# The minimum of the features on GpSimd, and the gate folded into the normaliser, in an attention-and-MoE kernel

## Chip, core and metric

The kernel runs on one core of a Trainium2 chip. The metric is the device time of one execution in microseconds (us); less is better. The engines are TensorE (PE; PEld is its weight load), VectorE (DVE), ScalarE (ACT), GpSimd (POOL) and SyncE (SP), whose queue issues the DMAs. Each engine runs its instructions in the order of its own queue, and waits on semaphores for the others.

## What is computed

Inputs: q, k, v of shape (4, 8, 576, 64), a memory matrix M_prev per batch and head (64 x 64), its normaliser z_prev, a gate beta per head, and four weight matrices. Cut to what matters:

```python
a = softmax(causal(q @ k.T / 8))
local = a @ v
q_p = np.where(q > 0, q, np.exp(q) - 1.0) + 1.0        # the features
mem_norm = (q_p * z_prev).sum(-1) + 1e-06
mem_out = (q_p @ M_prev) / mem_norm
g = 1.0 / (1.0 + np.exp(-beta))
x = g * mem_out + (1 - g) * local                       # (2304, 512)
out = ((x @ w1) * (x @ w2)) @ w3 @ w_out
```

The features are max(q, 0) + exp(min(q, 0)). The factor g / mem_norm is applied to the features of each token before they are multiplied with M_prev, and (1 - g) to the rows of the softmax.

## The kernel before

Two heads make a pair; the 4 batches have 16 pairs, and `pair_step(p)` handles one. The list ORDER gives the order in which a step is written down: transposes of the softmax rows of pair p (t1 to t4b, `t_mm`, L245 and L255 on PE, copied out of PSUM on ACT in L268), the product of rows and values (`pv_mm`, L277), `fin` (L288 on ACT and L289 on DVE, which split the result into a high and a low part), and then for the next pair the scores (`s_all`, L216 on PE; row minima with the mask on DVE, L193), the exponentials (L226, ACT) and the normalisation (L230, L231, L235 on DVE). At each F in ORDER, `Fill` writes down a share of other matmuls: in batch 0 the product of w3 and w_out (L423), in later batches the MoE of the batch before (`gemm1`, L473, and `gemm2`, L493). In `gemm1` ACT scales one product out of PSUM (L479), DVE multiplies the other to it (L482), ACT makes a rounded high part (L484) and POOL the low part (L485). The conversion of the weights from 64 bits (`conv_stages`: L310 on ACT, L314 and L315 on DVE, L322 on ACT, L323 on DVE) runs during batch 0 and the start of batch 1. After the last pair the MoE of the last batch runs alone.

The written order is not the order on the engines. A planner takes the instructions as written, gives each a place on its engine by priority and by the moment at which it reckons it ready, and adds the semaphores; instructions under `high_priority` come earlier. So the memory steps of a pair run well ahead of the place where they are written.

The memory steps of a pair, which the change touches:

- `load_qn` fetches q in token layout into the tile qn (L141 to L143; two buffers) and z (L146; two buffers) through SP's queue. A buffer of qn is free when the last features of its pair have been written (L178); one of z, when L160 has read it.
- `mem_a`: ACT makes e = relu(-q) (L152) and then e = exp(-e) (L153). The tile e is 128 x 640 and has one buffer.
- `mem_b`: DVE makes the features qn = max(q, 0) + e (L158), POOL makes e = qn * z (L160).
- `mem_c`: DVE sums e per token and head (L166, 128 x 10), adds 1e-6 (L167), takes the reciprocal (L168) and multiplies by the gate g_sb (L172); POOL multiplies the features with this, into the columns behind the softmax rows (L175 into sm0, L178 into smx), where the transposes of the next step take them. Both wait until the transposes of the pair before have read these columns.
- `copy_qd` (L120, POOL) copies q and k of the first rows when their DMA has landed.

Before the first pair, ACT and DVE make g_sb = 1 / (1 + exp(-beta)) (L604, L606, L607) and gi = 1 + exp(beta), which goes into the softmax sums.

Of the kernel before, what the change touches and what calls it, by code (L numbers as in the profile page):

```python
# [12 lines left out]
ACTF = mybir.ActivationFunctionType  # L13
ALU = mybir.AluOpType
# [28 lines left out]
def attention_moe_kernel(  # L43
# [13 lines left out]
    nc = tc.nc  # L57
# [35 lines left out]
    g_sb = const.tile([128, H], F32, name="g_sb")  # L93
# [55 lines left out]
    def mem_a(p):  # L149
        t = qn_t[p]  # L150
        e = mem_p.tile([128, 5, 2, D], F32, tag="e", name="e")
        nc.scalar.activation(out=e, in_=t, func=ACTF.Relu, scale=-1.0)  # L152
        nc.scalar.activation(out=e, in_=e, func=ACTF.Exp, scale=-1.0)  # L153
        stat["e", p] = e

    def mem_b(p):
# [5 lines left out]
    def mem_c(p):  # L162
        t, e = qn_t.pop(p), stat.pop(("e", p))
        n = st_p.tile([128, 5, 2, 1], F32, tag="n", name="n")
        nf = n.rearrange("p t h o -> p (t h) o")
        nc.vector.tensor_reduce(out=nf, in_=e.rearrange("p t h d -> p (t h) d"), axis=AX.X, op=ALU.add)  # L166
        nc.vector.tensor_scalar(out=n, in0=n, scalar1=1e-6, scalar2=None, op0=ALU.add)  # L167
        nc.vector.reciprocal(out=n, in_=n)  # L168
        h0 = 2 * p % H
        n3 = n.rearrange("p t h o -> p t (h o)")  # L170
        gb = g_sb[:, h0:h0 + 2].rearrange("p (o h) -> p o h", o=1).to_broadcast([128, 5, 2])
        nc.vector.tensor_tensor(out=n3, in0=n3, in1=gb, op=ALU.mult)  # L172
        for a in range(2):
            r = slice(64 * a, 64 * a + 64)
            nc.gpsimd.tensor_tensor(out=sm0[r, 64:128], in0=t[r, 0, a], in1=n[r, 0, a].to_broadcast([64, D]), op=ALU.mult)  # L175
        for k, lo, q, o in ((1, 0, 384, 192), (3, 512, 640, 576)):
            d = smx[:, :, lo:lo + 2 * q].rearrange("p a (k q) -> p k a q", q=q)[:, :, :, o:o + D]
            nc.gpsimd.tensor_tensor(out=d, in0=t[:, k:k + 2], in1=n[:, k:k + 2].to_broadcast([128, 2, 2, D]), op=ALU.mult)  # L178
# [364 lines left out]
    def pair_step(p, F):  # L543
# [23 lines left out]
            pv=(1, lambda: pv_mm(p)),  # L567
            fin=(1, lambda: fin(p)),
            ma=(nx, lambda: mem_a(p + 1)),
            mb=(nx, lambda: mem_b(p + 1)),  # L570
            qd=(nx, lambda: copy_qd(p + 1)),
            mc=(nx, lambda: mem_c(p + 1)),
        )
        for t in ORDER:
# [15 lines left out]
        out=mask[:, 448:576], in_=mask[:, 448:576], pattern=[[-1, 128]], compare_op=ALU.is_ge,  # L590
# [13 lines left out]
    nc.scalar.activation(out=g_sb, in_=beta_sb, func=ACTF.Exp, scale=-1.0)  # L604
    nc.scalar.activation(out=gi, in_=beta_sb, func=ACTF.Exp)
    nc.vector.tensor_scalar(out=g_sb, in0=g_sb, scalar1=1.0, scalar2=None, op0=ALU.add)  # L606
    nc.vector.reciprocal(out=g_sb, in_=g_sb)  # L607
    nc.vector.tensor_scalar(out=gi, in0=gi, scalar1=1.0, scalar2=None, op0=ALU.add)
    gp = gi.rearrange("p (j a) -> p j a", a=2)
    for k in range(4):  # L610
# [26 lines left out]
    load_v(0)  # L637
    load_qn(1)
    mem_a(0)
    mem_b(0)  # L640
    mem_c(0)
    F.slot()
    for b in range(B):
# [41 lines left out]
```

## Time and profile before

| | |
|---|---|
| median of 3 runs | 559.87 us (559.64 to 559.92) |
| the profiled execution | 558.28 us, its span 556.5 us |
| PE busy | 530.4 us, 95% of the span |
| DVE busy | 277.6 us, 50% |
| ACT busy | 269.0 us, 48% |
| POOL busy | 128.6 us, 23% |
| mean granted PE clock | 0.987 |

The span runs from the first to the last instruction of one profiled execution. A share of the span is an average over stages that have different limits. In rows of a timeline, "[x <-Y]" says that the engine stood idle for x us before the instruction and that Y ended the wait; a wait for several semaphores is put down to the one that came last. In rows by line, the two numbers behind the bar are the busy time in us and the mean of one instruction in ns. An instruction that the engine starts while the one before is still draining overlaps with it in these rows. Spans on POOL are rough.

### The profile page before, as it was taken

What the parts mean: (1) busy time and instruction counts of PE and PEld (TensorE: products, weight loads), DVE (VectorE), ACT (ScalarE), POOL (GpSimd) and SP (SyncE); (2) the same over time, 40 slices, a digit from 0 to 9 for tenths busy, and PEclk for the clock granted to TensorE, in tenths of its full rate; (3) what the DMA queues carried; (4) which work ended last, traced back from release to release, by engine and by line L of the source; (5) the groups of instructions that cost most, each with busy time, mean ns of one, the idle gap of its engine ahead of it and who ended that gap; (6) DMA issues with size and microseconds to landing.
All of it is one profiled execution on the core that took longest, in us unless ns stands there. A gap on an engine that the chain in (4) does not pass through costs nothing.

```text
span 556.5 us, 9501 instructions
## 1 busy us (share of the span) xinstructions
PE 530.4 (95%) x3488; PEld 428.5 (77%) x3488; DVE 277.6 (50%) x887; ACT 269.0 (48%) x691; POOL 128.6 (23%) x216
## 2 busy tenths in 40 slices
PE   4889987898999999999999999999999999999997
PEld 2344544546898899889988988798979897998995
DVE  5975969869671818182717081725434251111111
ACT  5654857848664555454644454534535361220210
POOL 1120522122423024212321233112311220220210
PEclk9799989998999999999999999999999999999999
DMA  7994375653312221132112120302121100001001
GB/s 295 403 323 142 115 212 177 216 165 106 105 48 67 86 65 51 49 104 67 49 53 100 48 68 24 113 31 68 44 61 62 44 2 19 20 1 39 0 1 57
DMA packets 35741, 51.46 MB, mean 92 GB/s; under 512 B 13424, under 2 KB 25712, under 8 KB 34160
## 3 DMA queue, kind: packets, MB, share of 16 engines
q1 hardware_dynamic: 35696, 50.87, 28.3%
q8 instruction: 27, 0.44, 0.4%
q14 instruction: 18, 0.15, 0.1%
HBM read 46.14 MB, written 4.72 MB: 91 GB/s over the span
## 4 chain that ended last, share of the span: by engine, by line
PE 72%; DVE 10%; ACT 6%; DMA 4%; issue 4%; POOL 2%; SPq 2%; POOLq 0%; DVEq 0%; ACTq 0%
PE m L473 34%; PE m L493 18%; PE x L277 7%; PE s L245 6%; PE s L216 4%; DVE smx L235 3%; ACT smx L226 2%; DMA wst<-w 2%; PE m L423 2%; PE sx L216 2%; DVE smx L193 1%; DMA wst<-w_out 1%; ACT pt L268 1%; POOL e L160 1%; POOL smx L178 1%
## 5 line engine op out<-in xcount | busy, mean ns | idle before, releaser
L473 PE MATMUL m<-xs,wsp 128*128 128x288 f32 x1536 | 224.7, 300 | 0.4 <-ACT a L479 0.3
L473 PEld LDWEIGHTS m<-xs,wsp 128*128 128x128 f32 x1536 | 207.3, 188 | 3.4 <-ACT a L479 1.1
L485 POOL TENSOR_TENSOR ht<-a,ht 128x288 fp32r<-128x288 f32 (+2 forms) x96 | 59.2, 631 | 169.3 <-ACT ht L484 169.0
L226 ACT ACTIVATE smx<-smx,mx 128x320 f32<-128x320 f32 (+3 forms) x128 | 77.3, 605 | 41.0 <-DVE mx L193 40.7
L482 DVE SCALAR_TENSOR_TENSOR a<-m,a 128x288 f32<-128x288 f32 x64 | 29.1, 455 | 134.1 <-PE m L473 124.6
L493 PE MATMUL m<-wH,ht 128*128 128x512 f32 x288 | 95.3, 397 | 0.0
L268 ACT ACTIVATE pt<-s 128x512 f32<-128x512 f32 (+1 forms) x128 | 64.9, 559 | 55.8 <-PE s L245 55.7
L423 PE MATMUL m<-wo,w3s 128*128 128x512 f32 x128 | 65.1, 648 | 5.6 <-DVE w3s L315 4.1
L245 PE MATMUL s<-ident,smx 128*128 128x128 f32 x448 | 61.3, 273 | 7.6 <-DVE smx L235 5.8
L245 PEld LDWEIGHTS s<-ident,smx 128*128 128x128 f32 x448 | 52.1, 140 | 15.2 <-DVE smx L235 7.1
L493 PEld LDWEIGHTS m<-wH,ht 128*128 128x128 f32 x288 | 54.1, 188 | 11.4
L493 PE MATMUL m<-wL,ht 128*128 128x512 f32 x144 | 56.3, 391 | 0.0
L484 ACT ACTIVATE ht<-a 128x288 fp32r<-128x288 f32 (+2 forms) x96 | 31.2, 358 | 49.7 <-DVE a L482 49.7
L235 DVE TENSOR_SCALAR smx<-smx,sums 128x320 f32<-128x320 f32 (+3 forms) x128 | 52.5, 460 | 1.0
L423 PEld LDWEIGHTS m<-wo,w3s 128*128 128x128 f32 x128 | 24.7, 207 | 33.5 <-issue 22.1
L479 ACT ACTIVATE a<-m 128x288 f32<-128x288 f32 x64 | 26.0, 407 | 45.7 <-PE m L473 40.8
L160 POOL TENSOR_TENSOR e<-qn,z 128x640 f32<-128x640 f32 x16 | 24.8, 1551 | 96.9 <-DVE qn L158 50.0
L193 DVE CUSTOM_DVE_ANT_0 smx<-s,mask 128x320 f32<-128x320 f32 (+2 forms) x96 | 42.1, 486 | 9.1 <-PE s L216 9.1
L216 PE MATMUL s<-raw 64*128 64x320 f32 (+3 forms) x256 | 37.7, 413 | 4.5 <-DMA raw<-qkt 4.5
L289 DVE TENSOR_TENSOR xs<-x,xs 128x576 fp32r<-128x576 f32 x16 | 12.1, 756 | 58.0 <-ACT xs L288 57.8
L216 PEld LDWEIGHTS s<-raw 64*128 64x128 f32 x256 | 23.5, 195 | 19.6 <-issue 11.8
L277 PE MATMUL x<-pt,v 128*64 128x512 f32 (+3 forms) x256 | 38.4, 439 | 0.0
(63 smaller groups left out, 459.9 us busy)
## 6 DMA issues: line engine op xcount, KB each, us to landing
raw<-qkt SPq DMA_DIRECT2D x16, 576.0 KB, 3.8
wst<-w3t SPq DMA_DIRECT2D x8, 1024.0 KB, 9.1
wst<-w SPq DMA_DIRECT2D x16, 512.0 KB, 4.9
out<-o SPq DMA_DIRECT2D x18, 256.0 KB, 2.0
wst<-w_out SPq DMA_DIRECT2D x4, 1024.0 KB, 11.6
v<-v SPq DMA_DIRECT2D x16, 256.0 KB, 2.8
qn<-qn SPq DMA_DIRECT2D x16, 160.0 KB, 2.9
u<-v SPq DMA_DIRECT2D x32, 80.0 KB, 2.6
```

The lines of the kernel that those rows point to most:

```text
L193: nc.vector.tensor_tensor_reduce(out=sm[a][c][:, lo:hi] if c else sm0[:, 0:64], in0=x, in1=mask[:, S - KE[c] + lo:S - KE[c] + hi] if c els ...
L216: nc.tensor.matmul(y, lhsT=t[r, 0, 128 * c - 64:128 * c + 64], rhs=t[r, 1, lo:hi], start=True, stop=True)
L226: nc.scalar.activation(out=x, in_=x, func=ACTF.Exp, bias=mx, scale=-1.0, accum_out=sums_of(p)[:, k:k + 1])
L235: nc.vector.tensor_scalar(out=x, in0=x, scalar1=sums_of(p)[:, k:k + 1], scalar2=None, op0=ALU.mult)
L245: tr = lambda o, c, a, kc: nc.tensor.transpose(ps[:, o:o + 128], sm[a][c][:, 128 * kc:128 * kc + 128], ident)
L268: nc.scalar.activation(out=job[1], in_=job[0], func=ACTF.Copy)
L277: nc.tensor.matmul(x[64 * a:64 * a + 64, X0 + q0:X0 + q1], lhsT=vv[:, a, k] if k < 4 else uu[:, k - 4, a], rhs=pt[:, a, o:o + q1 - q0], st ...
L423: nc.tensor.matmul(ps, lhsT=w[:, 128 * kc:128 * kc + 128], rhs=wo[:, 512 * (kc % 2):512 * (kc % 2) + 512], start=(kc == 0), stop=(kc == 7))
L473: nc.tensor.matmul(ps[:, 0:U], lhsT=w[:, i, x, j], rhs=x_t[NC * b + j][:, xx, U * u:U * u + U], start=(k == 0), stop=(k == 11))
L484: nc.scalar.activation(out=hbuf(f, 0)[:, p:p + c], in_=a[:, o:o + c], func=ACTF.Copy)
L485: nc.gpsimd.tensor_tensor(out=hbuf(f, 1)[:, p:p + c], in0=a[:, o:o + c], in1=f32(hbuf(f, 0)[:, p:p + c]), op=ALU.subtract)
L493: nc.tensor.matmul(ps, lhsT=hbuf(f, a)[:, p:p + 128], rhs=b[f], start=(k == 0), stop=(k == 23))
```

## The change

ACT's relu pass over the negated features is replaced by a minimum with zero on POOL, which writes the same tile; the exponential then takes its input with its sign as it is. g_sb keeps 1 + exp(-beta), without the reciprocal; the normaliser is (sum + 1e-6) * (1 + exp(-beta)), in one DVE instruction, and the reciprocal is taken after that.

```diff
     def mem_a(p):
         t = qn_t[p]
         e = mem_p.tile([128, 5, 2, D], F32, tag="e", name="e")
-        nc.scalar.activation(out=e, in_=t, func=ACTF.Relu, scale=-1.0)
-        nc.scalar.activation(out=e, in_=e, func=ACTF.Exp, scale=-1.0)
+        nc.gpsimd.tensor_scalar(out=e, in0=t, scalar1=0.0, scalar2=None, op0=ALU.min)
+        nc.scalar.activation(out=e, in_=e, func=ACTF.Exp)
         stat["e", p] = e
...
         nc.vector.tensor_reduce(out=nf, in_=e.rearrange("p t h d -> p (t h) d"), axis=AX.X, op=ALU.add)
-        nc.vector.tensor_scalar(out=n, in0=n, scalar1=1e-6, scalar2=None, op0=ALU.add)
-        nc.vector.reciprocal(out=n, in_=n)
         h0 = 2 * p % H
         n3 = n.rearrange("p t h o -> p t (h o)")
         gb = g_sb[:, h0:h0 + 2].rearrange("p (o h) -> p o h", o=1).to_broadcast([128, 5, 2])
-        nc.vector.tensor_tensor(out=n3, in0=n3, in1=gb, op=ALU.mult)
+        nc.vector.scalar_tensor_tensor(out=n3, in0=n3, scalar=1e-6, in1=gb, op0=ALU.add, op1=ALU.mult)
+        nc.vector.reciprocal(out=n, in_=n)
...
     nc.vector.tensor_scalar(out=g_sb, in0=g_sb, scalar1=1.0, scalar2=None, op0=ALU.add)
-    nc.vector.reciprocal(out=g_sb, in_=g_sb)
```

## Rows read from the trace of the kernel before

**Rows 1.** Table by stage: stretch, its length, busy us (instructions) of each engine.

```profile
core 0: us, PE busy (x) PEld busy (x) DVE busy (x) ACT busy (x) POOL busy (x), PEclk, DMA share, GB/s
0.00:143.76 143.76, 121.68 (x586) 69.03 (x588) 115.27 (x340) 95.34 (x217) 33.22 (x52) 0.95 0.63 212
143.76:474.70 330.94, 330.60 (x2403) 286.37 (x2403) 150.83 (x526) 159.27 (x435) 81.28 (x141) 1.00 0.20 58
```

**Rows 2.** Waits of PE: who waited for whom, us in total, times, longest.

```profile
PE s L245 <- DVE smx L235: 5.8, 4, 2.5
...
PE s L245 <- POOL smx L178: 1.2, 1, 1.2
```

**Rows 3.** Instructions by line and form: busy us, mean ns, idle before.

```profile
L152 ACT ACTIVATE e<-qn 128x640 f32<-128x640 f32 x16 | 11.8, 735 | 36.9 <-DMA qn<-qn 36.9
...
L160 POOL TENSOR_TENSOR e<-qn,z 128x640 f32<-128x640 f32 x16 | 24.8, 1551 | 96.9 <-DVE qn L158 50.0 <-ACT wo L310 18.7 <-DMA raw<-qkt 11.1
...
L167 DVE TENSOR_SCALAR n<-n 128x10 f32<-128x10 f32 x16 | 2.9, 178 | 0.3
```

**Rows 4.** Chain of waits of the first 140 us: start us, us, piece.

```profile
14.41 0.11 DVE g_sb L607
...
28.64 0.08 DVE n L167
...
101.78 0.63 ACT e L152
...
127.38 0.18 DVE n L167
```

**Rows 5.** Waits of ACT and POOL over the whole span, columns as in group 2.

```profile
ACT e L152 <- DMA qn<-qn: 36.9, 11, 4.5
...
ACT a L479 <- POOL ht L485: 4.8, 9, 0.6
...
POOL e L160 <- DVE qn L158: 50.0, 7, 14.9
```

**Rows 6.** POOL's simpler instructions, by line and form, columns as in group 3.

```profile
L588 POOL MEMSET mask<- 128x576 bf16 x1 | 0.6, 578 | 0.3 <-POOLq L678 0.3
L589 POOL TENSOR_SCALAR_AFFINE_SELECT mask<-mask 128x128 bf16<-128x128 bf16 x1 | 0.3, 292 | 0.0
```

**Rows 7.** Timeline of ACT and DVE: start us, us, instruction, idle before it.

```profile
51.98 0.73 ACT L152 ACTIVATE e<-qn 128x640 f32<-128x640 f32 x1
...
122.46 0.74 ACT L152 ACTIVATE e<-qn 128x640 f32<-128x640 f32 x1 [4.30 <-DMA qn<-qn]
...
124.05 0.83 DVE L158 SCALAR_TENSOR_TENSOR qn<-qn,e 128x640 f32<-128x640 f32 x1 [4.61 <-ACT e L153]
```

**Rows 8.** DVE beside POOL's product (timeline); lines L230, L315: ns min/median/max.

```profile
23.76 1.85 DVE L235 TENSOR_SCALAR smx<-smx,sums 128x576 f32<-128x576 f32 x1
...
26.13 0.51 DVE L235 TENSOR_SCALAR smx<-smx,sums 128x576 f32<-128x576 f32 x1
...
55.33 0.62 DVE L193 CUSTOM_DVE_ANT_0 smx<-s,mask 128x448 f32<-128x448 f32 x1
...
114.03 1.94 DVE L315 SCALAR_TENSOR_TENSOR wp<-wst,wp 128x512 uint32<-128x512 uint32 x1
...
L230 DVE SCALAR_TENSOR_TENSOR sums<-sums,gis x48: 115/156/1441, 15.7 to 451.9; 128x2 f32<-128x2 f32 x32, 128x5 f32<-128x5 f32 x16
...
L315 DVE SCALAR_TENSOR_TENSOR wp<-wst,wp x16: 676/688/1944, 75.0 to 144.2; 128x512 uint32<-128x512 uint32 x16
```

**Rows 9.** Timeline of DVE, first pair: the sum and the product with the gate.

```profile
26.89 0.81 DVE L166 TENSOR_REDUCE n<-e 128x10 f32<-128x640 f32 x1
...
30.23 0.16 DVE L172 TENSOR_TENSOR n<-n,g_sb 128x10 f32<-128x10 f32 x1
```

**Rows 10.** Timeline of POOL and ACT, in both stages.

```profile
107.25 1.02 POOL L120 COPY qd<-raw 64x64 f32<-64x64 f32 x2 [15.60 <-DMA raw<-qkt]
...
318.89 0.74 ACT L152 ACTIVATE e<-qn 128x640 f32<-128x640 f32 x1 [4.46 <-DMA qn<-qn]
...
321.20 1.18 POOL L485 TENSOR_TENSOR ht<-a,ht 128x288 fp32r<-128x288 f32 x1 [6.59 <-ACT ht L484]
```

## Prediction

> **What bounds the kernel now.** I read the page first, then a table by stage, then who waits for whom, then the chain of waits. The busy shares of the page name TensorE (PE) alone, but an average over the span hides the point. The table by stage [rows 1] cuts the span at 143.76 us, where the fifth pair's P@V begins and MoE matmuls fill PE; from 474.70 us on MoE work alone is left, which the change doesn't touch. In the first stage PE is busy 121.68 of 143.76 us, so it idles 22.1 us; in the second it is busy 330.60 of 330.94 us. There the most that can be had is 0.3 us, and something is lost only if a new wait reaches PE. So the change is decided in the first stage, which holds seven of the sixteen memory steps. VectorE (DVE) is busy 115.27 us of it, ScalarE (ACT) 95.34 us, GpSimd (POOL) 33.22 us [rows 1], and the longest total of PE's waits, 5.8 us, names a DVE line, L235 [rows 2]. DVE is the engine nearest to its limit; the one that the change relieves most is ACT, the one that it loads is POOL.
>
> **The relu pass.** Sixteen relu passes of 735 ns leave ACT, 11.8 us in all [rows 3]; the exponential stays. Nine of them lie in the stage that PE fills and count for nothing. Of the seven others the chain of waits of the first 140 us holds one, the piece of 0.63 us at 101.78 us [rows 4]: -0.6 us. Elsewhere ACT stood still anyway: it idled 36.9 us in all in front of relus, for the DMA of the features [rows 5]. That wait isn't removed. It moves to POOL's queue, and ACT then waits for POOL in front of the exponential.
>
> **The minimum on POOL.** The trace has no such instruction, so I bound it. From below: a POOL write without any input, 578 ns for 576 elements. From above: the product with z, 1551 ns [rows 3], which has the shape of the minimum and reads two inputs. The nearest row in kind is the select, with one input: 292 ns for 128 elements [rows 6]; five times that, 1.46 us for 640 elements, is too much, because part of the 292 ns is paid once. I take the middle of the bounds, an estimate of 1.05 us. Sixteen of them add 16.8 us to POOL, which has room.
>
> At 122.46 us the order of the work is laid bare. ACT waits 4.30 us for the DMA, then come relu and exponential, and DVE, idle for 4.61 us, starts L158 at 124.05 us [rows 7]; the chain comes out of this at L167 at 127.38 us [rows 4]. There the minimum takes the relu's place one for one: 1.05 - 0.74 = +0.3 us, with bounds -0.2 and +0.8 us.
>
> **What the minimum collides with.** While POOL ran the product with z, some DVE instructions beside it grew. L235 of 576 columns took 1.85 us at 23.76 us, against 0.51 us; L230 went up to 1.44 us against a median of 0.16 us; L315 took 1.94 us at 114.03 us against a median of 0.69 us. L193, which reads PSUM, kept its 0.62 us beside a product [rows 8]. In the first stage four of the seven products did this (the fourth is an L235 again), 1.34 + 0.85 + 1.28 + 1.25 = 4.7 us together, or 0.44 us for each microsecond of product (7 x 1.55 = 10.9 us). The Trainium skill states a rule behind this in "SBUF — State Buffer", section "Who interferes with whom": GpSimd and VectorE share a pair of ports as an exclusive lock, and of two instructions that want it the later one blocks whole; on VectorE's side these are instructions in a two-port mode or with two SBUF inputs. The rows agree with it, and it speaks against this change.
>
> Seven minima of 1.05 us at a rate of 0.44 make 3.2 us of DVE time; the other bound is nothing, as ACT's passes had none of this. Three of the seven relus, from the one at 51.98 us to the one at 122.46 us [rows 7], run beside L193 or an idle DVE, and I expect the minima where the relus were; so I keep 4/7, 1.8 us. DVE is busy 0.8 of the stage [rows 1], and I let that share of it reach the path: +1.4 us.
>
> **The small DVE operations.** L167, 178 ns [rows 3], goes, and the product with the gate becomes one fused operation of the kind of L230, 0.16 us [rows 8], as long as the plain one was. L167's pieces in the chain are four, 0.08 to 0.18 us and 0.48 us together; the gate's own reciprocal, which goes too, stands there with 0.11 us [rows 4]: -0.6 us. In the first pair DVE runs weight conversions between the links: from the end of L166 (27.70 us) to the end of L172 (30.39 us) lie 2.7 us [rows 9], and PE then waits 1.2 us for POOL's L178 behind them [rows 2]. One of three links less would be 0.9 us, so up to 0.8 us beyond what is counted, and at least nothing if DVE merely runs the same conversions earlier; I take 0.4 us. One more pair, the third, repeats the pattern at about half that length: up to 0.4 us, of which I take 0.3 us. Together -0.7 us.
>
> **The stage that PE fills.** POOL's queue now holds a minimum that waits for a DMA, and the low halves L485 are queued behind it; ACT's L479 waits for those to free its tile, and PE for L479. What hides this is seen in one step: the relu starts at 318.89 us, when the DMA has landed, and the next L485 starts at 321.20 us, when ACT has made its input [rows 10]. A minimum of 1.05 us fits between. L479 waited for L485 4.8 us in all, at most 0.6 us at once [rows 5]. I cost this at nothing; if that cover is gone, a fourth rival below has its price.
>
> **Sum.** -0.6 - 0.6 - 0.7 + 0.3 + 1.4 = -0.2 us. The profiled execution took 558.28 us with a span of 556.5 us, so 1.8 us lie around the span; the median of the three runs is 559.87 us, 0.3% more. Applied to the median: 559.7 us.
>
> **The rivals.** *The relief comes through and the port costs nothing* (faster): the minima fall where DVE reads PSUM or waits. Then the gains of 1.9 us stand with at most 0.3 us against them, -1.6 us or more; with the full 0.8 and 0.4 us for the links it is -2.4 us with nothing against it. In the middle 557.9 us. For it: three relus run in such places. Against it: DVE is busy four fifths of the stage.
>
> *The port decides* (slower): the minima hold DVE as the products do, all 3.2 us reach the path, the minimum costs 0.8 us more than the relu at 122.46 us, and the links give only the 0.6 us: 3.2 + 0.8 - 0.6 - 0.6 = +2.8 us, 562.7 us. Its place is the first stage; it decides from some 2.7 us of lengthened DVE instructions on the path (1.6 us of net gain without it, and 1.1 us more). For it: four products in seven did so. Against it: the minimum is shorter.
>
> *POOL's order* (the change does not do what it says, as ACT is not freed): a planner sets the order on every engine anew, and POOL works in order. At 107.25 us L120 had waited 15.60 us for a DMA [rows 10]. Were a minimum planned behind such a wait, the exponential that follows the relu of 101.78 us would start after 108.8 us, some 6 us late, with ACT's next softmax passes behind it; less a microsecond of slack +5 us, 564.9 us. Against it: relu and minimum wait for the same DMA, so the minimum is ready first.
>
> *The filled stage turns* (slower): if nine waits of POOL reach PE with 0.5 us each, +4.5 us, 564.4 us. Against it: POOL already waits in order for L158, 50.0 us in seven waits [rows 5], and PE idles 0.3 us in that stage all the same.
>
> **How the numbers follow.** The forecast has 0.38, relief without a port's cost 0.34, the port 0.18, POOL's order 0.06, the filled stage 0.04. The range takes in the bounds of the first three cases, 559.87 - 2.5 = 557.3 us (rounded) to 562.7 us; beyond it lie the last two and the far ends of the others. A measurement of this kernel can tell about 0.2%, 1.1 us, from no change; the forecast falls within that, the first rival is faster, the other three slower: 0.34, 0.38 and 0.28.
>
> **What would show it.** ACT's busy time should fall by some 11.8 us and POOL's rise by 10 to 25 us; DVE's should hardly fall, because the 2.8 us of L167 come back as lengthened L235, L230, L314 or L315 beside the minima. The port rival would show as more DVE instructions of over a microsecond and more than 22 us of PE idle time ahead of the filled stage; the relief as none of these beside the minima and less than 21 us. A minimum that starts long after its DMA landed would show POOL's order; PE idle for more than a microsecond in the filled stage the fourth rival. A minimum outside 0.58 to 1.55 us, or a chain of the first stage that has left DVE and ACT for the DMA queues, would make my terms wrong.

## The result, and the profile after

The changed kernel takes 566.83 us (median of 5 runs, 565.47 to 567.27), the kernel before 559.64 us beside it; the ratio is 1.0117, with a 95% interval of 1.0092 to 1.0142. It is slower by some 7 us (by the ratio 0.0117 x 559 = 6.5 us), beyond the range of the prediction, and on the side that got the smallest chance. In its profiled execution the span is 563.8 us against 556.5 us, so 7.3 us are to be found.

The busy time of each engine, from the page of the changed kernel:

```profile
PE 533.3 (95%) x3488; PEld 429.3 (76%) x3488; DVE 276.0 (49%) x870; ACT 260.0 (46%) x675; POOL 156.7 (28%) x232
```

ACT lost 9.0 us and POOL gained 28.1 us. (The sixteen relus are 11.8 us by line; this list counts time in which two instructions of an engine overlap once.) Line numbers of the changed kernel: L152 is now the minimum, L153 and L158 are as before; behind L170 they are lower by one or two: L166 is still the sum, L170 the fused operation, L171 the reciprocal, L174 and L177 are POOL's products, L192 the score minima, L288 the subtraction of `fin`, L472 to L484 `gemm1`. The table by stage, cut where the fifth pair's P@V begins and where the last one ends, as in [rows 1]:

```profile
0.00:148.52 148.52, 123.29 (x584) 69.54 (x584) 115.75 (x332) 90.46 (x210) 45.47 (x59) 0.94 0.61 205
148.52:482.50 333.98, 332.73 (x2409) 287.57 (x2409) 149.49 (x518) 155.12 (x426) 97.13 (x150) 1.00 0.19 58
```

The first stage is 4.8 us longer: PE idles 25.2 us of it (22.1 before) and is busy 1.6 us longer at a granted clock of 0.94 (0.95 before). The stage that PE fills is 3.0 us longer, 333.98 against 330.94 us: 0.9 us of it is PE idle time, and most of the rest is that six matmuls of `gemm1` ran in it that ran after it before (1104 against 1098); what is left behind that stage is 0.5 us shorter. The waits of PE that answer to [rows 2]:

```profile
PE s L244 <- DVE smx L234: 5.2, 5, 2.9
...
PE sx L215 <- DVE xs L288: 5.1, 2, 4.5
...
PE s L201 <- DVE mx L192: 2.6, 1, 2.6
```

PE's wait for POOL in the first pair has shrunk from 1.2 to 0.6 us (now for L174), and in second place stands one that was 2.2 us before: scores that wait for `fin`. The minimum and its neighbour by line, which answer to [rows 3]:

```profile
L152 POOL TENSOR_SCALAR e<-qn 128x640 f32<-128x640 f32 x16 | 29.7, 1857 | 59.3 <-DMA qn<-qn 57.3 <-DVE sums L229 2.1
...
L160 POOL TENSOR_TENSOR e<-qn,z 128x640 f32<-128x640 f32 x16 | 24.7, 1547 | 43.2 <-DVE qn L158 42.1 <-DVE sums L230 1.1
```

With one input the minimum takes 1857 ns, longer than the product with two inputs of the same shape, which I had taken as its upper bound. The waits around it, which answer to [rows 5]:

```profile
POOL e L152 <- DMA qn<-qn: 57.3, 14, 9.6
...
DVE qn L158 <- ACT e L153: 34.5, 12, 6.5
...
ACT e L153 <- POOL e L152: 31.7, 14, 5.7
```

ACT stands 31.7 us in its queue at the exponential, for POOL. DVE stands 34.5 us at the features L158, behind that exponential; in the kernel before it was 5.8 us in five waits:

```profile
DVE qn L158 <- ACT e L153: 5.8, 5, 4.6
```

One place where this reaches PE, from the timeline of the changed kernel after the second pair's P@V:

```profile
69.09 1.19 POOL L177 TENSOR_TENSOR smx<-qn,n 128x256 f32<-128x256 f32 x2
...
70.24 1.80 POOL L152 TENSOR_SCALAR e<-qn 128x640 f32<-128x640 f32 x1
...
72.08 0.74 ACT L153 ACTIVATE e<-e 128x640 f32<-128x640 f32 x1 [4.11 <-POOL e L152]
...
72.85 0.82 DVE L158 SCALAR_TENSOR_TENSOR qn<-qn,e 128x640 f32<-128x640 f32 x1 [3.99 <-ACT e L153]
...
73.76 1.53 POOL L160 TENSOR_TENSOR e<-qn,z 128x640 f32<-128x640 f32 x1 [1.71 <-DVE qn L158]
...
75.32 0.82 DVE L166 TENSOR_REDUCE n<-e 128x10 f32<-128x640 f32 x1 [1.65 <-POOL e L160]
...
76.39 0.75 DVE L288 TENSOR_TENSOR xs<-x,xs 128x576 fp32r<-128x576 f32 x1
...
77.20 1.90 PE L215 MATMUL sx<-raw 64*128 64x512 f32 x4 [4.49 <-DVE xs L288]
```

The minimum is the fourth pair's, and was planned behind the third pair's features (L177), so it starts late; ACT stands 4.11 us for it, DVE 3.99 us for ACT, and once more 1.65 us for POOL's product at the sum. P@V had ended at 70.9 us. But ACT's half of `fin` stood behind the exponential and ran at 73.28 us, DVE's half, L288, stood behind the sum L166, and PE waited 4.49 us for it. Nothing needs the fourth pair's features soon, since its P@V begins at 118.4 us. What was ready stood behind them in the engines' queues. The same place in the kernel before, where the waits are there too, but shorter:

```profile
68.40 0.82 DVE L158 SCALAR_TENSOR_TENSOR qn<-qn,e 128x640 f32<-128x640 f32 x1 [0.54 <-ACT e L153]
...
73.34 1.13 PE L216 MATMUL sx<-raw 64*128 64x512 f32 x4 [1.62 <-DVE xs L289]
```

Not all of that wait is lost time: the changed kernel is 0.99 us late at the start of the second pair's P@V, 2.23 us at the third's, 4.33 us at the fourth's and 4.83 us at the fifth's. The step from the third to the fourth has another place of the kind, where the order itself has changed. In the kernel before, the features stood behind the score minima on DVE:

```profile
109.05 1.10 PE L245 MATMUL s<-ident,smx 128*128 128x128 f32 x8 [1.67 <-DVE smx L235]
...
112.85 0.81 DVE L158 SCALAR_TENSOR_TENSOR qn<-qn,e 128x640 f32<-128x640 f32 x1
```

In the changed kernel the planner put them ahead of seven score minima, and DVE stands there for the exponential, while the exponential waits for the minimum at 102.90 us:

```profile
105.73 0.83 DVE L158 SCALAR_TENSOR_TENSOR qn<-qn,e 128x640 f32<-128x640 f32 x1 [2.47 <-ACT e L153]
...
112.55 1.10 PE L244 MATMUL s<-ident,smx 128*128 128x128 f32 x8 [2.93 <-DVE smx L234]
```

So a wait of DVE and a new order, which puts ready work behind that wait, come together here.

The place that stands in [rows 7] at 122.46 us, in the timeline of the changed kernel:

```profile
126.57 1.80 POOL L152 TENSOR_SCALAR e<-qn 128x640 f32<-128x640 f32 x1 [7.53 <-DMA qn<-qn]
...
128.41 0.74 ACT L153 ACTIVATE e<-e 128x640 f32<-128x640 f32 x1 [5.72 <-POOL e L152]
...
129.18 0.82 DVE L158 SCALAR_TENSOR_TENSOR qn<-qn,e 128x640 f32<-128x640 f32 x1 [5.70 <-ACT e L153]
```

From the landing of the features to L158 lie 2.61 us, 1.59 us before: +1.02 us, where the prediction had +0.3 with an upper bound of +0.8. And the chain of waits of the changed kernel holds the minimum where [rows 4] hold the relu of 101.78 us, and in the stage that PE fills:

```profile
102.90 2.04 POOL e L152
...
152.30 1.82 POOL e L152
...
240.30 1.82 POOL e L152
```

### The profile page after: what moved, and what is told of

It is laid out like the page before. It is cut to its first block, busy times and chain, and to the rows that moved or that the text cites. A ratio compares the mean times of both kernels' runs of the same rounds, so it can differ in the third digit from the quotient of the medians.

```text
span 563.8 us, 9472 instructions
## 1 busy us (share of the span) xinstructions
PE 533.3 (95%) x3488; PEld 429.3 (76%) x3488; DVE 276.0 (49%) x870; ACT 260.0 (46%) x675; POOL 156.7 (28%) x232
## 4 chain that ended last, share of the span: by engine, by line
PE 72%; DVE 11%; ACT 5%; DMA 4%; POOL 4%; issue 2%; SPq 1%; POOLq 0%; DVEq 0%; ACTq 0%
PE m L472 33%; PE m L492 16%; PE s L244 7%; PE x L276 7%; PE s L215 4%; DMA qn<-qn 3%; PE m L422 3%; DVE smx L234 2%; DVE smx L192 2%; ACT smx L225 2%; POOL e L152 2%; PE sx L215 2%; DMA wst<-w_out 1%; POOL smx L177 1%; DVE qn L158 1%
## 5 line engine op out<-in xcount | busy, mean ns | idle before, releaser
L472 PE MATMUL m<-xs,wsp 128*128 128x288 f32 x1536 | 225.6, 300 | 1.2 <-ACT a L478 0.6
L472 PEld LDWEIGHTS m<-xs,wsp 128*128 128x128 f32 x1536 | 207.5, 188 | 5.0 <-ACT a L478 1.6
L484 POOL TENSOR_TENSOR ht<-a,ht 128x288 fp32r<-128x288 f32 (+2 forms) x96 | 59.1, 630 | 158.9 <-ACT ht L483 158.6
L483 ACT ACTIVATE ht<-a 128x288 fp32r<-128x288 f32 (+2 forms) x96 | 31.2, 358 | 49.5 <-DVE a L481 49.5
L478 ACT ACTIVATE a<-m 128x288 f32<-128x288 f32 x64 | 26.1, 408 | 44.7 <-PE m L472 39.5
L152 POOL TENSOR_SCALAR e<-qn 128x640 f32<-128x640 f32 x16 | 29.7, 1857 | 59.3 <-DMA qn<-qn 57.3
L192 DVE CUSTOM_DVE_ANT_0 smx<-s,mask 128x320 f32<-128x320 f32 (+2 forms) x96 | 41.7, 482 | 9.0 <-PE s L215 9.0
L288 DVE TENSOR_TENSOR xs<-x,xs 128x576 fp32r<-128x576 f32 x16 | 12.1, 756 | 57.6 <-ACT xs L287 57.6
L276 PE MATMUL x<-pt,v 128*64 128x256 f32 (+3 forms) x256 | 38.6, 439 | 0.0
```

What stands on the lines that cost most here:

```text
L152: nc.gpsimd.tensor_scalar(out=e, in0=t, scalar1=0.0, scalar2=None, op0=ALU.min)
L192: nc.vector.tensor_tensor_reduce(out=sm[a][c][:, lo:hi] if c else sm0[:, 0:64], in0=x, in1=mask[:, S - KE[c] + lo:S - KE[c] + hi] if c els ...
L276: nc.tensor.matmul(x[64 * a:64 * a + 64, X0 + q0:X0 + q1], lhsT=vv[:, a, k] if k < 4 else uu[:, k - 4, a], rhs=pt[:, a, o:o + q1 - q0], st ...
L472: nc.tensor.matmul(ps[:, 0:U], lhsT=w[:, i, x, j], rhs=x_t[NC * b + j][:, xx, U * u:U * u + U], start=(k == 0), stop=(k == 11))
L484: nc.gpsimd.tensor_tensor(out=hbuf(f, 1)[:, p:p + c], in0=a[:, o:o + c], in1=f32(hbuf(f, 0)[:, p:p + c]), op=ALU.subtract)
```

## The experiments

Each ratio is to the kernel before on the same chip, with its 95% interval. The two columns behind it are, in one profiled execution, how much later than before the P@V of the fifth and the sixteenth pair began (143.69 and 462.96 us before); they tell the first stage from the second.

| kernel | median us | ratio | pair 5 | pair 16 |
|---|---|---|---|---|
| changed kernel | 566.83 | 1.0117 (1.0092 to 1.0142) | +4.83 | +6.90 |
| gate_only | 556.61 | 0.9954 (0.9930 to 0.9977) | -0.44 | -1.09 |
| gate_again | 557.07 | 0.9972 (0.9953 to 0.9991) | -0.35 | -1.01 |
| min_only | 565.82 | 1.0111 (1.0066 to 1.0155) | +5.97 | +8.81 |
| exp_first | 563.61 | 1.0089 (1.0060 to 1.0117) | +3.00 | +4.31 |
| min_dve | 560.19 | 1.0019 (0.9996 to 1.0041) | +2.03 | +2.91 |
| relu_twice | 558.88 | 0.9984 (0.9964 to 1.0004) | +1.21 | +2.83 |
| extra_pass | 561.21 | 1.0048 (1.0026 to 1.0070) | +3.85 | +3.76 |
| min_part | 564.48 | 1.0099 (1.0072 to 1.0126) | +1.53 | +5.99 |
| gate_late | 557.85 | 0.9971 (0.9950 to 0.9992) | -2.34 | +0.44 |
| late_part | 557.73 | 0.9982 (0.9966 to 0.9998) | -2.61 | +0.18 |
| late_exp | 560.06 | 1.0010 (0.9994 to 1.0026) | -2.14 | +0.76 |
| late_sum | 561.06 | 1.0041 (1.0027 to 1.0054) | -0.53 | +2.47 |
| late_twice | 579.67 | 1.0380 (1.0356 to 1.0404) | +7.81 | +21.79 |

Single executions of one kernel spread by up to 6 us (gate_only: 553.83 to 559.69), so the ratios decide, and the columns show where. A difference of ratios times 559 us is called a price below; by the intervals of its two ratios a price is good to some 1.5 us either way.

Three theories stood against each other. Lateness: the features come about a microsecond later, and ACT and DVE stand in order behind them. Length: the price goes with the minimum's 1.86 us against the relu's 0.74 us. POOL itself: what costs is that POOL is occupied, that its order shifts, or that its accesses hold DVE.

### The two parts apart

*The gate alone.* Against the changed kernel:

```diff
-        nc.gpsimd.tensor_scalar(out=e, in0=t, scalar1=0.0, scalar2=None, op0=ALU.min)
-        nc.scalar.activation(out=e, in_=e, func=ACTF.Exp)
+        nc.scalar.activation(out=e, in_=t, func=ACTF.Relu, scale=-1.0)
+        nc.scalar.activation(out=e, in_=e, func=ACTF.Exp, scale=-1.0)
```

> Only the gate is folded in ahead of the reciprocal; relu and exponential stay on ScalarE as before. Theory A (the loss comes from the minimum on GpSimd, 1.80 us where the relu took 0.74 us): this part alone gives what the prediction reckoned for it, -1.3 to 0 us against the kernel before, 558.3 to 559.7 us. Rival B (the fold makes the planner set another order, and that order costs): +2 us or more, 561.6 us or above.

It takes 556.61 us, by the ratio 2.6 us faster than the kernel before: more than theory A reckoned, and rival B is out. The timeline of its first pair, DVE and POOL, answers to [rows 9]:

```profile
27.26 0.81 DVE L166 TENSOR_REDUCE n<-e 128x10 f32<-128x640 f32 x1
...
28.93 0.15 DVE L170 SCALAR_TENSOR_TENSOR n<-n,g_sb 128x10 f32<-128x10 f32 x1
...
29.94 0.20 DVE L171 RECIPROCAL n<-n 128x10 f32<-128x10 f32 x1
...
30.22 1.05 POOL L174 TENSOR_TENSOR sm<-qn,n 64x64 f32<-64x64 f32 x2 [4.56 <-DVE n L171]
...
31.33 0.33 PE L254 MATMUL s<-ident,sm 128*128 128x128 f32 x1 [0.63 <-POOL sm L174]
```

From the end of the sum to the end of the last link lie 2.07 us, 2.69 us before: one link less is 0.6 us, and PE waits 0.63 us there in place of 1.22 us.

*The minimum alone.* Against the changed kernel, the gate's part as in the kernel before:

```diff
+        nc.vector.tensor_scalar(out=n, in0=n, scalar1=1e-6, scalar2=None, op0=ALU.add)
+        nc.vector.reciprocal(out=n, in_=n)
...
-        nc.vector.scalar_tensor_tensor(out=n3, in0=n3, scalar=1e-6, in1=gb, op0=ALU.add, op1=ALU.mult)
-        nc.vector.reciprocal(out=n, in_=n)
+        nc.vector.tensor_tensor(out=n3, in0=n3, in1=gb, op=ALU.mult)
...
+    nc.vector.reciprocal(out=g_sb, in_=g_sb)
```

> Only the minimum moves to GpSimd; the gate's three small operations stay. On GpSimd the order of the third and fourth pair differs from that of the changed kernel: here the minimum of the fourth pair is planned ahead of the third pair's features, there behind them. Theory A1 (each microsecond of the minimum's length counts, whatever the order): +7 to +8.5 us against before, that is the whole loss and the fold's gain on top. Theory A2 (some 3 us of the loss come from that one place in GpSimd's order): +3 to +5 us, and the first product with the values of the fifth pair starts 2 to 4 us earlier than in the changed kernel. Rival B (the fold's order): 0 to +2 us.

It loses 6.2 us by the ratio, as much as the whole change within the intervals, although here the minimum of the fourth pair runs ahead of the third pair's features. That lies between the ranges of A1 and A2, and A2's sign is missing: the fifth pair's P@V starts 1.1 us later than in the changed kernel, not 2 to 4 us earlier. So POOL's order at the one place shown above, at 70.24 us, is not what the loss hangs on.

*The gate alone, a second time*, with a profile of its own; the kernel is the same.

> The folded gate alone, a second time and with a profile of its own: whether its gain over the kernel before is there again, and whether the granted clock of the first stage is what carries it. In the first profile three stretches of the first stage ran at the lower clock where the kernel before had four, PE's busy time was 2.9 us less, and its idle time 1.8 us more. If the fold itself carries the gain, 556 to 557.5 us again, with PE idle less in the first stage in at least one of the profiles; if the clock carries it, the time goes with the number of low stretches, near 555.5 us with three and 557.5 us or more with four.

It takes 557.07 us, and the gain is there again. One sign of the expectation failed: PE is idle 24.0 and 22.6 us in the first stage in the two profiles, in neither less than the 22.1 us before. But the clock does not carry the gain. The ten executions had a mean granted clock of 0.989, the kernel before beside them 0.989 too, and they were faster all the same; and counted in steps of 1 us all three profiles have three low stretches in the first stage (the expectation gives four for the kernel before). In gate_only the mean was 0.992 against 0.989, so its larger gain may be in part the clock. Mean of the two ratios: 0.9963. Against it the minimum's price in the changed kernel is (1.0117 - 0.9963) x 559 = 8.6 us; from min_only against the kernel before it is 6.2 us, the same within the intervals.

### What the minimum costs: its length, its engine, or who stands behind it

*The exponential first, the minimum behind it.* Against the changed kernel:

```diff
-        nc.gpsimd.tensor_scalar(out=e, in0=t, scalar1=0.0, scalar2=None, op0=ALU.min)
-        nc.scalar.activation(out=e, in_=e, func=ACTF.Exp)
+        nc.scalar.activation(out=e, in_=t, func=ACTF.Exp)
+        nc.gpsimd.tensor_scalar(out=e, in0=e, scalar1=1.0, scalar2=None, op0=ALU.min)
```

> As the changed kernel, but ScalarE takes the exponential of the features as they come, and GpSimd then takes the minimum of that with one; the result is the same, the minimum keeps its length and its port. Theory C (ScalarE standing in order behind the minimum, with the copy of the product and the softmax passes queued behind, is the cost): most of the loss goes, 0 to +2.5 us against before. Theory A (VectorE's sum of the features and the addition stand in order behind the chain, which is as long as before): +5 to +8 us.

It takes ACT's wait behind the minimum away, and leaves DVE 15.5 us in thirteen waits at L158 (34.5 us in the changed kernel). The ratio falls by 0.0028, 1.6 us, no more than the intervals leave to chance, and stands 5.0 us above the kernel before: theory C is out, theory A at the lower end of its range.

*The minimum on DVE.*

```diff
-        nc.gpsimd.tensor_scalar(out=e, in0=t, scalar1=0.0, scalar2=None, op0=ALU.min)
+        nc.vector.tensor_scalar(out=e, in0=t, scalar1=0.0, scalar2=None, op0=ALU.min)
```

> As the changed kernel, but the minimum is taken by VectorE. Theory A: the chain from the DMA to the features is shorter than with the relu (an estimate of 0.4 us from L314, which is of this kind, against 0.74 us), and seven of these add 3 us of work to VectorE in the first stage: -1 to +3 us against before. Rival D (the loss is from GpSimd's port, as VectorE's instructions stand behind the minimum): the loss goes wholly and the relief of ScalarE comes through, -3 to 0 us. If the order that is planned anew is what counts, any value from -3 to +8 us.

There it takes 490 ns and still costs (1.0019 - 0.9963) x 559 = 3.1 us. Against the kernel before that is +1.1 us, within theory A's range and outside rival D's. It is no clean price of one more engine in the chain, since DVE has sixteen instructions more and the order is planned anew. ACT stands 22.8 us in nine waits for the minimum. PE stands twice for ACT's product L478: 1.50 us at 152.78 us, where L478 stood behind an exponential that had waited 3.53 us for the minimum, and 4.57 us at 134.78 us, where it stood behind softmax passes and other work. How the 3.1 us divide is open.

*The relu twice on ACT*, the gate folded, against gate_only:

```diff
         nc.scalar.activation(out=e, in_=t, func=ACTF.Relu, scale=-1.0)
+        nc.scalar.activation(out=e, in_=e, func=ACTF.Relu)
```

> The kernel with the gate folded and the relu on ACT, with a second relu on ACT over the same tile between the first and the exponential: the chain from the features' loading to the sum L166 grows by one ACT pass of about 0.7 us (735 ns in the kernel before), GpSimd gets nothing, and DVE's shared port meets nothing new. Lateness theory (what costs is that the features come about a microsecond later and ACT and DVE stand in order behind them): it adds 16 passes of 0.7 us to the chain, so 4 to 7 us over the folded gate alone (556.6 us), near 561 to 563 us. GpSimd theory (what costs is that GpSimd is occupied and its order shifts, or that its accesses slow DVE): 0 to +2 us over the folded gate alone, near 557 to 558 us.

0.7 us more of chain, without POOL, costs 1.2 us by the ratios, which their intervals do not tell from nothing. That is below what lateness alone was said to give and within what the GpSimd theory allowed.

*A pass on POOL that nobody waits for*, behind the sum, against gate_only:

```diff
         nc.vector.tensor_reduce(out=nf, in_=e.rearrange("p t h d -> p (t h) d"), axis=AX.X, op=ALU.add)
+        nc.gpsimd.tensor_scalar(out=e, in0=e, scalar1=0.0, scalar2=None, op0=ALU.min)
```

> The kernel with the gate folded and the relu on ACT, with a pass of the minimum on GpSimd over e put behind the sum L166, where nobody reads its result: GpSimd's occupation and its accesses beside DVE as with the minimum in the relu's place, and no longer chain to the features. GpSimd theory (occupation and order of GpSimd, and the port): 5 us or more over the folded gate alone (556.6 us), since the features L174 and L177 and the tile e then stand behind 1.8 us of GpSimd. Lateness theory: 0 to +2 us over the folded gate alone, near 557 to 559 us.

It costs 4.8 us, just under what the GpSimd theory said, so 1.9 us of POOL in each pair are not free even off the chain. Nearly all of it, 4.3 us in the profiles, lies ahead of the fifth pair, and much of it at one place. The timeline of PE there in extra_pass, and the table of that stretch:

```profile
111.25 1.10 PE L245 MATMUL s<-ident,smx 128*128 128x128 f32 x8 [2.19 <-DVE smx L235]
...
112.30 2.72 PE L245 MATMUL s<-ident,smx 128*128 128x128 f32 x12
```

```profile
110.00:119.00 9.00, 7.75 (x39) 5.59 (x41) 8.59 (x18) 6.78 (x14) 3.62 (x5) 0.81 0.51 170
```

The same instructions in gate_only, and the same stretch:

```profile
109.03 1.10 PE L244 MATMUL s<-ident,smx 128*128 128x128 f32 x8 [1.54 <-DVE smx L234]
...
110.08 1.47 PE L244 MATMUL s<-ident,smx 128*128 128x128 f32 x12
```

```profile
110.00:119.00 9.00, 9.00 (x67) 5.82 (x66) 8.90 (x17) 5.94 (x12) 3.84 (x5) 1.00 0.52 173
```

Between the third and the fourth pair extra_pass falls 3.5 us behind gate_only, and 1.9 us of it lie here: a wait that was 0.65 us longer was followed by a fall of the granted clock from the higher of its two levels (2.4 GHz) to the lower (1.2 GHz): twelve transposes took 2.72 us in place of 1.47 us. So here PE lost more than the wait's own length. The length of the wait is not shown to be the cause: at 112.55 us of the changed kernel PE waited 2.93 us, and the granted clock from 112 to 118 us was 1.00.

*The minimum on two of five token blocks.* Against the changed kernel; the minimum of the other three blocks is left out:

```diff
-        nc.gpsimd.tensor_scalar(out=e, in0=t, scalar1=0.0, scalar2=None, op0=ALU.min)
-        nc.scalar.activation(out=e, in_=e, func=ACTF.Exp)
+        nc.gpsimd.tensor_scalar(out=e[:, 0:2], in0=t[:, 0:2], scalar1=0.0, scalar2=None, op0=ALU.min)
+        nc.scalar.activation(out=e[:, 2:5], in_=t[:, 2:5], func=ACTF.Exp)
+        nc.scalar.activation(out=e[:, 0:2], in_=e[:, 0:2], func=ACTF.Exp)
```

> The change with the minimum on GpSimd for two of the five token blocks only (256 of 640 columns), and the exponential in two passes; the minimum of the other three blocks is left out, so the features of positive queries differ from the reference there. The minimum then takes about 0.75 us (0.4 of 1.86 us), as long as the relu that it replaces. Length theory (the price is the minimum's length, 1.86 us against the relu's 0.74): most of the price goes, 0 to +3 us over the folded gate alone, 557 to 560 us. Theory of the hand-over (the price is that one more engine stands in the chain, and that GpSimd's own order holds the minimum up): at least half of the price stays, 562 us or more.

The minimum now takes 902 ns, and the kernel 564.48 us: most of the price stays. It has moved. In the first stage this kernel is only 1.5 us late, and then it loses 1.4 to 1.5 us at each of three places of the stage that PE fills. One of them, from its timeline (L159 are the features, L161 the product, L167 the sum):

```profile
263.34 0.85 POOL L152 TENSOR_SCALAR e<-qn 128x256 f32<-128x256 f32 x1 [2.45 <-DMA qn<-qn]
...
264.22 0.42 ACT L154 ACTIVATE e<-e 128x256 f32<-128x256 f32 x1 [0.59 <-POOL e L152]
...
264.67 0.83 DVE L159 SCALAR_TENSOR_TENSOR qn<-qn,e 128x640 f32<-128x640 f32 x1 [5.21 <-ACT e L154]
...
267.19 0.82 DVE L167 TENSOR_REDUCE n<-e 128x10 f32<-128x640 f32 x1 [1.02 <-POOL e L161]
...
267.92 0.45 DVE L482 SCALAR_TENSOR_TENSOR a<-m,a 128x288 f32<-128x288 f32 x1
...
268.43 0.79 PE L473 MATMUL m<-xs,wsp 128*128 128x288 f32 x4 [1.03 <-DVE a L482]
```

DVE was given the product L482 of the MoE behind the sum, and the sum waits for POOL; PE stands 1.03 us for L482. With another length the planner laid out another order, and the order has its own price. So here, and in each comparison above that leaves the planner free, length and order are mixed. The chain is not longer here than with the relu: three fifths of the exponential run beside the minimum.

### With DVE's place held

Five kernels hold the place that matters most. The features L158 of each pair are queued on DVE behind the last score minimum of the pair before:

```diff
-        nc.vector.scalar_tensor_tensor(out=t, in0=t, scalar=0.0, in1=e, op0=ALU.max, op1=ALU.add)
+        with tc.issue_after(stat["red", max(p - 1, 0)].ins):
+            nc.vector.scalar_tensor_tensor(out=t, in0=t, scalar=0.0, in1=e, op0=ALU.max, op1=ALU.add)
...
-        nc.vector.tensor_tensor_reduce(
+        stat["red", p] = nc.vector.tensor_tensor_reduce(
```

> The change with DVE's features L158 of each pair queued behind the last score minimum L192 of the pair before: DVE then no longer stands at L158 ahead of score minima that are ready. Theory of DVE's standing (what is lost in the stage of the pairs is DVE waiting in order for the exponential behind the minimum): half or more of the 7 us goes, 559 to 563 us. Theory of lateness at the consumers (the features themselves are late for the product P@V): the features come later still, so 566 us or more.

It takes 561.06 us: by the ratios 4.2 of the 6.5 us are gone, though the minimum is no shorter (1.97 us in the mean, 1.86 us in the changed kernel). DVE's waits for the exponential at the features, 34.5 us in the changed kernel, are gone from the list of waits altogether; ACT's for the minimum are still there:

```profile
ACT e L153 <- POOL e L152: 25.9, 12, 6.4
```

The place of the first timeline above, in late_sum (L159 are the features, L289 is `fin`, L193 are the score minima):

```profile
69.95 1.80 POOL L152 TENSOR_SCALAR e<-qn 128x640 f32<-128x640 f32 x1
...
71.78 0.74 ACT L153 ACTIVATE e<-e 128x640 f32<-128x640 f32 x1 [4.11 <-POOL e L152]
...
74.17 0.75 DVE L289 TENSOR_TENSOR xs<-x,xs 128x576 fp32r<-128x576 f32 x1
...
74.98 1.17 PE L216 MATMUL sx<-raw 64*128 64x512 f32 x4 [2.57 <-DVE xs L289]
...
79.75 0.82 DVE L159 SCALAR_TENSOR_TENSOR qn<-qn,e 128x640 f32<-128x640 f32 x1
```

The minimum starts as late as in the changed kernel and ACT stands as long, but DVE goes on: `fin` runs at 74.17 us in place of 76.39 us, PE waits 2.57 us for it in place of 4.49 us, the score minima follow, and the features come at 79.75 us, long before the P@V that needs them (117.08 us).

*The control, without the minimum* (the same edit on gate_only):

> The folded gate alone (relu on ACT), with DVE's features L158 of each pair queued behind the last score minimum of the pair before, as in the run that did this with the minimum on GpSimd (561.06 us). It is that run's control. If DVE's later place is worth 5 us by itself, whatever stands ahead of it, this gives 550 to 553 us. If it is worth something only where DVE would stand behind a long minimum, this gives 555.5 to 558 us, about the folded gate alone (556.6 us).

The place is worth nothing by itself over the whole kernel: 557.85 us. In the profile that is a sum of two things: gate_late begins the fifth pair 1.9 us earlier than gate_only, and the sixteenth 1.5 us later. So the minimum's price with DVE's place held is (1.0041 - 0.9971) x 559 = 3.9 us, 8.6 us with the planner free. The difference, 4.7 us, is about half of the price (by the intervals some 2 us more or less). It takes both to pay it: the long minimum in front of the exponential, and L158 queued early on DVE with ready work behind it. What else the planner moved when L158 was held back is not separated from this.

*Length, with the place held.* late_part has the minimum of two blocks as in min_part (the other three blocks' minimum is left out), late_twice takes the minimum twice:

```diff
         nc.gpsimd.tensor_scalar(out=e, in0=t, scalar1=0.0, scalar2=None, op0=ALU.min)
+        nc.gpsimd.tensor_scalar(out=e, in0=e, scalar1=0.0, scalar2=None, op0=ALU.min)
```

> The change with DVE's features L158 queued behind the last score minimum of the pair before, and the minimum on GpSimd for two of the five token blocks only (about 0.8 us; the other three blocks' minimum is left out). Length theory (with DVE's place held, the minimum's length sets what is left of the price): 557 to 559 us, half or less of the way from the folded gate with the same place of L158 to the 561.06 us of the full minimum. Hand-over theory: 560.5 us or more, as with the full minimum.

> The change with DVE's features L158 queued behind the last score minimum of the pair before, and the minimum on GpSimd taken twice in a row (about 3.7 us). Length theory: what the first minimum costs there is paid again, 564 to 567 us. Slack theory (with DVE's place held the chain to the features has slack, and length hardly counts): 561 to 563 us. Order theory (what a length changes is above all the order that is laid out for the engines): anything between 558 and 567 us, without an even step from none to one to two minima.

A minimum of 1.0 us costs 0.6 us, one of 2.0 us 3.9 us, two in a row, 3.8 us, 22.9 us. Length counts, then, but not evenly: near the relu's length it is free within the intervals (there the exponential is split, too, and part of it does not wait), and with each further microsecond it costs more. None of the three expectations of late_twice had this. The waits of ACT in late_twice, where L153 and L154 are the second minimum and the exponential:

```profile
ACT e L154 <- POOL e L153: 50.8, 15, 8.3
```

50.8 us in fifteen waits, 25.9 us in late_sum: with DVE out of the way, ACT is the one that stands.

*The exponential first, with the place held*: the edits of exp_first and late_sum together.

> The exponential first on ACT, then the minimum with one on GpSimd, and DVE's features L158 queued behind the last score minimum of the pair before: the chain keeps the same links and GpSimd the same work as with the minimum ahead (561.06 us), but neither ACT nor DVE stands behind the minimum. Its control, with no minimum on GpSimd and the same place of L158, took 557.85 us. If ACT's standing behind the minimum is what is left of the price there (3.2 us), this gives 557.5 to 559 us; if the chain's length or GpSimd's occupation is, 560.5 to 562 us.

560.06 us, between the two expectations. By the ratios ACT's standing is 1.7 us of the 3.9 us, and 2.2 us stay with the chain's length and POOL; in the profiled executions, where pair 16 begins at +0.76 us against +0.44 us of the control and +2.47 us of late_sum, nearly all of it was ACT. How the last 2 us divide between the chain's length and POOL is open.

## Why the prediction was wrong

*What bounds the kernel.* Right: most of the loss, 4.8 of 7.3 us, is in the first stage, where PE's idle time grew to 25.2 us, past the 22 us that I had set as the mark of a slower kernel. The mark itself was no good: gate_only and gate_again idle 24.0 and 22.6 us there and are faster.

*The relu pass, -0.6 us.* This is the first step that failed. I took the chain's piece of 101.78 us out, and put nothing in its place. The minimum stands at the same spot of the chain with 2.04 us: not -0.6 but +1.4 us.

*The minimum's length, 1.05 us, with bounds of 0.58 and 1.55 us.* Mis-sized, and outside its bounds: 1.86 us. That the product with two inputs had to be longer was a guess about the engine, which no row of before carried. At 122.46 us it made +1.02 us in place of +0.3 us.

*The minimum on the path at one place only.* This is the step that cost most. The [rows 5] show POOL waiting 50.0 us for L158 and ACT waiting 36.9 us for the DMA, and I read them as slack: who waits anyway loses nothing. But an engine that waits in order holds up what is queued behind it. While ACT waited for the DMA on its own, DVE stood at L158 for 5.8 us; with POOL between, DVE stands there for 34.5 us, with score minima and `fin` behind it. I had also expected each step where it was, and at 105.73 us the planner had moved L158 ahead of seven score minima. late_sum and its control show what DVE's place behind the minimum is worth: 4.7 of the minimum's 8.6 us.

*The port, +1.4 us from 1.8 us of lengthened DVE instructions.* Mis-sized, as a sum. In the first stage DVE is busy 115.75 us; in the two profiles of the fold alone, with as many DVE instructions there (332), it is busy 115.53 and 114.92 us. So the minimum adds 0.2 to 0.8 us of DVE time, not 1.8 us. Beside the minima DVE instructions did grow: at 58.75 us an L229 took 0.64 us against a median of 0.16 us. The Trainium skill's rule that GpSimd and VectorE share a pair of ports as an exclusive lock ("SBUF — State Buffer", section "Who interferes with whom") agrees with that. But beside POOL's products fewer grew than before: three took over a microsecond, in place of four, and none beside a minimum. Nor is lengthened DVE time by itself the loss: in late_sum DVE is busy 290.7 us, 14.7 us more than in the changed kernel, and the kernel is 4.2 us faster by the ratios.

*The small DVE operations, -1.3 us.* Right in sign, and in the first pair 0.6 us of links against the 0.4 us I took. Alone the fold gave 2.6 and 1.6 us by its two ratios. Where the rest of it lies is open; one profile of each does not tell it.

*The filled stage at nothing.* Wrong by about 1 us: PE idles 1.25 us there (0.3 us before). The cover that I named was real, but it was for a minimum of 1.05 us. At 325.30 us of the changed kernel the minimum ran 1.81 us, ACT stood 2.39 us for it with L483 and L478 behind it, and PE waited 0.35 us.

*The rivals.* POOL's order named a true mechanism, in-order standing behind a minimum, at about the right size (564.9 us), but with the wrong cause: it wanted the minimum behind a wait of POOL's own. Its sign that a minimum starts long after its DMA landed was seen at 70.24 us, and min_only loses as much without that one. It had a chance of 0.06, because I asked only whether the minimum would be late, and not what ACT and DVE would do while it ran. The port rival had the right sign in PE's idle time, though not its other one, more DVE instructions of over a microsecond, and the wrong reason.

## What to carry to other kernels

Before a step is handed to another engine, write down for every later link of its chain what is queued behind that link on its engine, and whether a planner may put more there: a wait moves along the chain, and each engine of it then stands in order, even where the chain's result is wanted much later. If the hand-over is needed, hold the next engine's part back behind work that is ready, and run a control with that order alone. Split a change of two parts: here the small one was a gain of some 2 us by itself, of which nothing shows beside the minimum (6.2 us lost without the fold, 6.5 us with it).

## What the runs showed of the hardware

A minimum with a constant on POOL, one input of 128 x 640 floats, takes 1.86 us in the mean of the changed kernel (1.80 to 2.34 us); the product of two such tiles takes 1.55 us. On 256 columns it takes 0.84 us undisturbed, so it goes by size at some (1.81 - 0.84) / 384 = 2.5 ns a column. On DVE the same minimum took 0.49 us. A wait of TensorE of 2.19 us was followed by matmuls at the lower clock in extra_pass; after one of 1.54 us in gate_only and one of 2.93 us in the changed kernel the granted clock stayed at the higher level. So the length of the wait does not decide it by itself.
